# Two more K tiles turned by DMA, another set turned by VectorE, and side work and weight loads moved: one attention kernel on one Trainium2 core

## The chip, the cores and the metric

The kernel runs on one core of one Trainium2 chip. The time is device microseconds from the start to the end of the program. Eleven runs of the kernel before had a median of 185.6 us (184.96 to 186.39). One further execution was recorded by the hardware profiler; it took 186.5 us, of which 183.6 us lie between its first and its last instruction (its span). All times of the trace count from the start of that span.

In what follows "turn" means transposing a K tile. TensorE (PE in the profile) multiplies matrices, ScalarE (ACT) computes the exponentials, VectorE (DVE) and GpSimd (POOL) copy and move, SyncE (SP) issues nearly all DMAs.

## What is computed

Attention over a window of a K/V cache, with a projection in front (`wq`) and one behind (`wo`). All data is bfloat16.

```python
B, Sq, D = 8, 32, 1024
Hq, Hkv, Sk, Dh = 32, 4, 8192, 128
W = min(4096, max(256, Sk // 4))              # 2048
rep = Hq // Hkv                               # 8 query heads share one K/V head
q = (x @ wq).reshape(B, Sq, Hq, Dh).transpose(0, 2, 1, 3)
k = jnp.repeat(k_cache[:, :, Sk - W:, :], rep, axis=1)
v = jnp.repeat(v_cache[:, :, Sk - W:, :], rep, axis=1)
p = softmax(einsum("bhqd,bhkd->bhqk", q, k) * Dh ** -0.5)
o = einsum("bhqk,bhkd->bhqd", p, v)
out = o.transpose(0, 2, 1, 3).reshape(B, Sq, Hq * Dh) @ wo
```

The kernel reads 16.8 MB of K, 16.8 MB of V, 8.4 MB of `wq` and 8.4 MB of `wo`.

## The kernel before

**Units, chunks, slots.** A unit is one pair of batch and K/V head: 32 units, numbered 0 to 31, all eight batches of head 0 first. A unit has 256 queries (8 heads by 32 positions) and 2048 keys. Its keys are taken in four chunks of four key tiles (128 keys each), so the main loop (`run`, L445) has 128 chunks. Their number is also called the slot: chunk `c` of unit `u` is slot `4u + c`.

**One slot on TensorE.** Four score matmuls (`s_ps`, L467: 128 keys by 256 queries each); then the eight matmuls of probabilities by V (`o_ps`, L478) of the chunk two slots earlier; then the side work that a plan puts into this slot. ScalarE turns each chunk's scores into `pT` with one exponential of 128 by 1024 (L469). There are two score buffers and two output accumulators, so TensorE can run at most two chunks ahead of ScalarE. V is copied by VectorE into a wider tile `va` with a column of ones (`va_copy`, L409), so that the sum of the softmax comes out of the same matmul. When a unit is done, `finish_unit` (L411) takes the reciprocal, scales (two instructions, L420) and transposes (L422) into `OT`, all on VectorE.

**Four ways to turn K.** The score matmul needs K with the head dimension on the partitions. `load_k` (L178) and the plan choose per unit:

- units 0 to 4 (`PE_T`, L24): a plain load of 512 KB, then 16 transposes on TensorE (`k_pieces`, L224; L236) and two VectorE copies out of PSUM (L238); unit 0 is turned in `start`;
- units 5, 8, 11, ... 29 (`V_T`, L26): a plain load, four block transposes on VectorE (L251), then 16 moves of 32 by 512 (`kv_pieces`, L241). The last number of an entry of `V_T` says how many of the 16 moves are GpSimd's (L261): 12 for unit 5, 16 for the others; VectorE makes the rest (L259). The first number says behind which unit's loads the plain load is issued, the middle ones in which slots the block transposes and the moves stand;
- the other 18 units: two transposing DMAs of 256 KB each (L196), the first eight key tiles and the last eight, one before V's load and one behind it.

**Loads.** All these DMAs go through SyncE's one queue in the order in which `load_unit` (L207) issues them: K, V, K's second half, then the plain K loads that `V_T` ties to this unit, then the weight pieces that `W_AT` (L28) ties to it. `load_unit` stands in the program five units ahead of use, but SyncE does not follow the slots: it goes on as fast as its waits on buffers and on the queue let it. V has 6 buffers, turned K of the transposing DMA 5, weight tiles 6.

**Weights and projections.** A weight piece is 512 KB, half of a tile; there are 28 behind the start (12 of `wq`, 16 of `wo`), listed in the order of use (L332 to L338). A tile of `wq` holds four of the eight row groups `c` of all eight heads of one K/V head, so that each contiguous run in memory is 1024 elements, 2 KB. The projection of the next head group's queries is side work: 16 pieces of four matmuls (`q_pieces`, L267), a VectorE copy after every second one (L278); `Q_SLOTS` (L30) says over which slots they are spread evenly. The output projection of a finished head group is 16 pieces of two matmuls (`o_pieces`, L282), spread by `O_SLOTS` (L31); pieces planned for slots from 128 on run after the loop.

**The start.** `start` (L312) loads x and the eight row groups of `wq` of head group 0, and multiplies each with all eight heads when it has landed (L375). For row groups 0 to 5 all 256 queries are done at once; for 6 and 7 (`Q_CUT`, L19) only the first 128, and the other half follows in slots 0 and 1 of the loop (`q_rest`, L401).

What moves and what stays can be read in these lines of the plan:

```python
for ui, (_, s0, s1, s2, _) in V_T.items():
    blocks, moves = self.kv_pieces(ui)
    for k, p in enumerate(blocks):
        plan[s0[k]].append(p)
    spread(moves, s1, s2)
```

Of the kernel before, what the change touches and what calls it, by code (L numbers as in the profile page):

```python
# [9 lines left out]
ALU = mybir.AluOpType  # L10
# [5 lines left out]

RL_LIMIT = 1.0e22
RL_MIN = 1.0e-10
Q_CUT = 6  # L19
N_WARM = (8, 0, 0)  # L20
VA_ROW = 160
V_HALVES = 30

PE_T = (0, 1, 2, 3, 4)  # L24

V_T = {5: (2, (5, 6, 8, 10), 10, 17, 12),  # L26
       **{u: (u - 4, range(4 * u - 16, 4 * u - 12), 4 * u - 13, 4 * u - 4, 16) for u in (8, 11, 14, 17, 20, 23, 26, 29)}}
W_AT = (3, 3, 4, 4, 8, 8, 9, 9, 11, 12, 13, 13, 14, 15, 16, 16, 18, 19, 19, 20, 22, 22, 23, 24, 25, 26, 28, 28)  # L28

Q_SLOTS = {1: (17, 31), 2: (38, 54), 3: (69, 83)}  # L30
O_SLOTS = {0: (54, 71), 1: (84, 101), 2: (99, 123), 3: (124, 143)}  # L31


@with_exitstack
# [70 lines left out]
class Fast:  # L105
# [50 lines left out]
    def load_wq(self, g, half, cuts=(2, 2)):  # L156
# [8 lines left out]
                                   in_=self.wq[:, g * GW:(g + 1) * GW].rearrange("(p c) n -> p c n", p=P)[:, c0:c0 + n, :])  # L165
        return [lambda i=sum(cuts[:k]), n=n: piece(i, n) for k, n in enumerate(cuts)]

    def load_wo(self, gq):

        def piece(i):  # L170
            if i == 0:
                self.wo_t[gq] = self.wp.tile([self.P, 4, self.D], BF16, name="wo_sb", tag="w")
            r0 = gq * 4 * self.Dh
            self.nc.sync.dma_start(out=self.wo_t[gq][:, 2 * i:2 * i + 2, :],
                                   in_=self.wo[r0:r0 + 4 * self.Dh, :].rearrange("(p c) n -> p c n", c=4)[:, 2 * i:2 * i + 2, :])
        return [lambda i=i: piece(i) for i in range(2)]
# [30 lines left out]
    def load_unit(self, ui):  # L207

        if ui < len(self.units):
            if ui not in V_T:  # L210
                self.load_k(ui, None if ui in PE_T else 0)
            self.load_v(ui, self.nc.sync)
            if ui not in V_T and ui not in PE_T:
                self.load_k(ui, 1)
        for u, at in V_T.items():
            if at[0] == ui:
                self.load_k(u)
        for p, at in zip(self.weights, W_AT):
            if at == ui:
                p()  # L220

# [17 lines left out]
    def kv_pieces(self, ui):  # L241


        nc, P, KT = self.nc, self.P, self.KT
        st = {}

        def blocks(i):
            if i == 0:
                st["kb"] = self.kbp.tile([P, KT, P], BF16, name="kb")
            sl = slice(i * KT // 4, (i + 1) * KT // 4)  # L250
            nc.vector.transpose(out=st["kb"][:, sl, :], in_=self.k_raw[ui][:, sl, :])  # L251

        def move(k, d):
            if k == d == 0:
                self.kT[ui] = self.kvt.tile([P, KT, P], BF16, name="kTv", tag="kv")
            out = self.kT[ui][d * 32:(d + 1) * 32, :, k * 32:(k + 1) * 32]
            in_ = st["kb"][k * 32:(k + 1) * 32, :, d * 32:(d + 1) * 32]
            if d >= V_T[ui][4] // 4:
                nc.vector.tensor_copy(out=out, in_=in_)  # L259
            else:  # L260
                nc.gpsimd.tensor_scalar(out=out, in0=in_, scalar1=1.0, scalar2=1.0, op0=ALU.mult, op1=ALU.mult)  # L261
        return [lambda i=i: blocks(i) for i in range(4)], [lambda k=k, d=d: move(k, d) for k in range(4) for d in range(4)]
# [4 lines left out]
    def q_pieces(self, g):  # L267
        nc, P, DC = self.nc, self.P, self.DC
        st = {}

        def piece(hl, i):
            if i == 0:
                st["ps"] = self.ps_m.tile([P, 512], FP32, name="q_ps", tag="m")
            for c in range(i * DC // 2, (i + 1) * DC // 2):
                nc.tensor.matmul(st["ps"][:, 0:self.NQ], lhsT=self.wq_t[g, i][:, c % (DC // 2), hl * P:(hl + 1) * P],  # L275
                                 rhs=self.xT[:, c, :], start=(c == 0), stop=(c == DC - 1))
            if i == 1:
                nc.vector.tensor_copy(out=self.q_view(g)[:, :, hl, :],  # L278
                                      in_=st["ps"][:, 0:self.NQ].rearrange("p (b s) -> p b s", b=self.B))
        return [lambda h=h, i=i: piece(h, i) for h in range(self.rep) for i in range(2)]  # L280

    def o_pieces(self, g, t, cuts=(512, 512), st=None):  # L282

# [28 lines left out]
    def start(self):  # L312
# [15 lines left out]
        self.load_k(0, 1)  # L328
        self.load_v(0, nc.sync)
        self.load_k(1)  # L330
        self.load_v(1, nc.sync)
        self.weights = []  # L332
        for g in range(self.Hkv):
            if g + 1 < self.Hkv:
                self.weights += self.load_wq(g + 1, 0) + self.load_wq(g + 1, 1)
            if g:
                self.weights += self.load_wo(2 * g - 2) + self.load_wo(2 * g - 1)
        self.weights += self.load_wo(2 * self.Hkv - 2) + self.load_wo(2 * self.Hkv - 1)  # L338
        for ui in range(2, 4):
            self.load_unit(ui)  # L340
        for v in self.va:
            nc.gpsimd.memset(v[:, :, self.Dh:self.VW], 1.0)
        nc.gpsimd.memset(self.ones_c[:, :], 1.0)
        def warm_up(n):
            for i in range(n):
                nc.tensor.matmul(warm[:, :], lhsT=one(1.0, [P, P], BF16), rhs=one(1.0, [P, 512], BF16), start=True, stop=True)
        warm_up(N_WARM[0])


        def x_turn(half, pl, tag):  # L350
# [4 lines left out]
            for i, copy in ((0, nc.vector.tensor_copy), (1, nc.scalar.copy)):  # L355
# [2 lines left out]

        x_turn(0, self.ps_m, "m")
        x_turn(1, self.ps_s, "s_ps")  # L360
        qs = [pl.tile([P, 2, self.NQ], FP32, name="q0_ps", tag=tag)
              for pl, tag in ((self.ps_o, "o_ps"), (self.ps_o, "o_ps"), (self.ps_m, "m"), (self.ps_m, "m"))]
        KT = self.KT
        tp = None

# [4 lines left out]
        def k_copy(half):  # L370
            sl = slice(half * KT // 2, (half + 1) * KT // 2)
            nc.vector.tensor_copy(out=self.kT[0][:, sl, :], in_=tp[:, sl, :])

        def q_mm(c, h, n0, n1):
            nc.tensor.matmul(qs[h // 2][:, h % 2, n0:n1], lhsT=self.wq_t[0, c // H][:, c % H, h * P:(h + 1) * P],  # L375
                             rhs=self.xT[:, c, n0:n1], start=(c == 0 and h % 2 == 0), stop=(c == self.DC - 1),
                             skip_group_check=True)

        for c in range(self.DC):
            for h in range(self.rep):  # L380
                q_mm(c, h, 0, P if c >= Q_CUT else self.NQ)
            if c == 0:
                warm_up(N_WARM[2])
                warm_sb = self.c1.tile([P, 8], BF16, name="warm_sb")
                nc.vector.tensor_copy(out=warm_sb[:, :], in_=warm[:, 0:8])
            if c == self.DC - 3:
                tp = self.ps_s.tile([P, KT, P], BF16, name="kf_ps", tag="s_ps")
                k_turn(0)
                k_copy(0)
        k_turn(1)  # L390

        def q_copy(eng, k, b0, b1):
            src = qs[k][:, :, :].rearrange("p h (b s) -> p b h s", b=self.B)[:, b0:b1, :, :]
            dst = self.q_view(0)[:, b0:b1, k * 2:(k + 1) * 2, :]
            (nc.vector.tensor_copy if eng == "v" else nc.scalar.copy)(out=dst, in_=src)
        for k, eng in ((0, "a"), (1, "v"), (2, "a"), (3, "v")):
            q_copy(eng, k, 0, 1)
        k_copy(1)
        self.va_copy(0)

        def q_rest(k):  # L401
            for h in (2 * k, 2 * k + 1):
                for c in range(Q_CUT, self.DC):
                    q_mm(c, h, P, self.NQ)
            q_copy("v", k, 1, self.B)
        self.q_rest = [lambda k=k: q_rest(k) for k in (0, 2, 3, 1)]

    def va_copy(self, ui):
        self.nc.vector.tensor_copy(out=self.va[ui % 3][:, :, 0:self.Dh], in_=self.v_sb[ui][:, :, :])  # L409
# [1 line left out]
    def finish_unit(self, ui, o_ps):  # L411
# [4 lines left out]
        if ui == len(self.units) - 1:  # L416
            self.check_units(ui, ui + 1)
        o_sb = self.ob.tile([P, QT_N, 4, 32], BF16, name="o_sb")
        for qt in range(QT_N):
            nc.vector.tensor_scalar(out=o_sb[:, qt, :, :], in0=o_ps[:, qt, 0:Dh].rearrange("p (i c) -> p c i", c=4),  # L420
                                    scalar1=rl[:, ui * QT_N + qt:ui * QT_N + qt + 1], scalar2=None, op0=ALU.mult)
        nc.vector.transpose(out=self.OT[:, g * QT_N:(g + 1) * QT_N, :, b * self.Sq:(b + 1) * self.Sq], in_=o_sb[:, :, :, :])  # L422
        if ui == len(self.units) - 2:
            self.check_units(0, ui + 1)
# [1 line left out]
    def side_plan(self):  # L426
# [4 lines left out]
        def spread(pieces, s0, s1):  # L431
            for k, p in enumerate(pieces):
                plan[s0 + (s1 - s0) * k // len(pieces)].append(p)
        for g, w in Q_SLOTS.items():
            spread(self.q_pieces(g), *w)
        for g, w in O_SLOTS.items():
# [8 lines left out]
    def run(self):  # L445
        nc, P, NCH, CJ, UQ, QT_N, KT = self.nc, self.P, self.NCH, self.CJ, self.UQ, self.QT_N, self.KT
        self.start()
        plan = self.side_plan()
        for i, p in enumerate(self.q_rest):
            plan[i // 2].append(p)  # L450
        pv_queue = []

        loads = {8: [4, 5, 6, 7], **{4 * (u - 5): [u] for u in range(8, len(self.units))}}
# [1 line left out]
        for ui, (b, g) in enumerate(self.units):  # L455
            nxt = self.k_pieces(ui + 1)
            va = self.va[ui % 3]
            if ui:
                self.va_copy(ui)
            q_u = self.QT[g][:, b * UQ:(b + 1) * UQ]  # L460
            acc = {}
            for c in range(NCH):
                for u in loads.get(ui * NCH + c, []):
                    self.load_unit(u)
                s_ps = self.ps_s.tile([P, CJ, UQ], FP32, name="s_ps")
                for jj in range(CJ):
                    nc.tensor.matmul(s_ps[:, jj, :], lhsT=self.kT[ui][:, c * CJ + jj, :], rhs=q_u, start=True, stop=True)  # L467
# [188 lines left out]
```

## Time and profile before

| what | value |
|---|---|
| median of 11 runs | 185.6 us (184.96 to 186.39) |
| the profiled execution | 186.5 us, span 183.6 us |
| granted TensorE clock | 1.00 throughout |
| TensorE busy | 178.6 us of the span, 97% |
| exponentials on ScalarE (L469) | 128 of 1025 ns; ScalarE busy 72% |
| VectorE, GpSimd busy | 114.8 us (63%), 94.7 us (52%) |
| moves on GpSimd (L261) | 140 of 670 ns |
| all DMA traffic | 51.72 MB, mean 282 GB/s |
| first score matmul | at 13.28 us |

The busy times come from the page's first part, the clock from the list of cores, the first score matmul from the timeline. A share of busy time is a mean over the whole span; the page's second part cuts the span into 40 slices of 4.59 us and gives a busy digit for each, where 9 means 90% or more. The DMA rows there are means over the core's 16 DMA engines. "To landing" is the time from the issue of a DMA to the moment its data is reported complete. Matmuls overlap each other in the pipeline, so the mean duration of one (220 ns for L478) is more than the distance from one to the next; that distance is read from the timeline, where eight matmuls of L478 move the next group on by 0.45 us.

### The profile page before, as it was taken

What the parts mean: (1) busy time and instruction counts of PE and PEld (TensorE: products, weight loads), DVE (VectorE), ACT (ScalarE), POOL (GpSimd) and SP (SyncE); (2) the same over time, 40 slices, a digit from 0 to 9 for tenths busy, and PEclk for the clock granted to TensorE, in tenths of its full rate; (3) what the DMA queues carried; (4) which work ended last, traced back from release to release, by engine and by line L of the source; (5) the groups of instructions that cost most, each with busy time, mean ns of one, the idle gap of its engine ahead of it and who ended that gap; (6) DMA issues with size and microseconds to landing.
All of it is one profiled execution on the core that took longest, in us unless ns stands there. A gap on an engine that the chain in (4) does not pass through costs nothing.

```text
span 183.6 us, 5041 instructions
## 1 busy us (share of the span) xinstructions
PE 178.6 (97%) x2041; PEld 153.6 (84%) x2057; DVE 114.8 (63%) x266; ACT 131.5 (72%) x133; POOL 94.7 (52%) x150
## 2 busy tenths in 40 slices
PE   8989999999999999999999999999999999999994
PEld 3889999999999999987878999988787888888843
DVE  0238899985585784685567558647755865365363
ACT  2208899777889777878787677787877888888800
POOL 2000009859939959929944980796299279600000
PEclk9999999999999999999999999999999999999999
DMA  5999999999998999999999999989999999990003
GB/s 189 336 411 406 399 401 377 147 271 385 263 341 264 338 294 321 402 255 246 373 384 234 377 390 232 249 318 383 250 370 342 219 279 264 223 213 0 0 31 91
DMA packets 52953, 51.72 MB, mean 282 GB/s; under 512 B 39744, under 2 KB 40256, under 8 KB 52928
## 3 DMA queue, kind: packets, MB, share of 16 engines
q1 hardware_dynamic: 52352, 50.90, 98.4%
q10 hardware_dynamic: 576, 0.49, 0.8%
q8 instruction: 15, 0.25, 0.5%
q14 instruction: 10, 0.08, 0.1%
HBM read 41.42 MB, written 0.52 MB: 228 GB/s over the span
## 4 chain that ended last, share of the span: by engine, by line
PE 93%; DMA 4%; SPq 1%; issue 1%; DVE 0%
PE o_ps L478 32%; PE s_ps L467 31%; PE op_ps L295 14%; PE q_ps L275 11%; DMA wq_sb<-in_wq_dram 4%; PE q_ps L375 2%; PE tp L236 2%; SPq L164 1%; PE kf_ps L368 1%; SPq L320 0%; DVE o_t L305 0%; PE cnt_ps L532 0%
## 5 line engine op out<-in xcount | busy, mean ns | idle before, releaser
L469 ACT ACTIVATE pT<-s_ps 128x1024 bf16<-128x1024 f32 x128 | 128.7, 1025 | 32.5 <-PE s_ps L467 31.5
L261 POOL TENSOR_SCALAR kTv<-kb 32x512 bf16<-32x512 bf16 x140 | 93.8, 670 | 64.2 <-PE s_ps L467 37.7
L478 PE MATMUL o_ps<-va,pT 128*128 128x129 bf16 x1024 | 78.8, 220 | 0.1
L478 PEld LDWEIGHTS <-pT 128*128 128x128 bf16 x1024 | 68.5, 98 | 3.1
L467 PE MATMUL s_ps<-QT,kT 128*128 128x256 bf16 x368 | 55.2, 272 | 0.2
L467 PEld LDWEIGHTS <-kT 128*128 128x128 bf16 x368 | 34.8, 98 | 10.3
L295 PE MATMUL op_ps<-wo_sb,OT 128*128 128x512 bf16 (+2 forms) x128 | 32.7, 352 | 0.6
L275 PE MATMUL q_ps<-xT,wq_sb 128*128 128x256 bf16 x192 | 28.2, 273 | 0.0
L409 DVE COPY va<-v_sb 128x2048 bf16<-128x2048 bf16 x32 | 25.3, 789 | 0.1
L251 DVE STREAM_TRANSPOSE kb<-k_raw 128x512 bf16<-128x512 bf16 x36 | 23.8, 684 | 0.0
L415 DVE RECIPROCAL RL_all<-o_ps 128x2 f32<-128x2 f32 x32 | 5.2, 164 | 27.5 <-PE o_ps L478 27.5
L467 PE MATMUL s_ps<-QT,kTv 128*128 128x256 bf16 x144 | 21.6, 272 | 0.0
L420 DVE TENSOR_SCALAR o_sb<-o_ps,RL_all 128x128 bf16<-128x128 f32 x64 | 19.5, 346 | 1.1
L467 PEld LDWEIGHTS <-kTv 128*128 128x128 bf16 x144 | 13.9, 98 | 5.1
L278 DVE CAST QT<-q_ps 128x256 bf16<-128x256 f32 x24 | 9.7, 406 | 13.4 <-PE q_ps L275 13.4
L275 PEld LDWEIGHTS <-wq_sb 128*128 128x128 bf16 x192 | 17.0, 98 | 1.2
L422 DVE STREAM_TRANSPOSE OT<-o_sb 128x256 bf16<-128x256 bf16 x32 | 14.3, 446 | 1.1
L295 PEld LDWEIGHTS <-OT 128*128 128x128 bf16 x144 | 11.4, 98 | 2.3 <-DVE OT L422 0.2
L302 DVE TENSOR_TENSOR oacc<-op_ps,oacc 128x512 f32<-128x512 f32 x8 | 5.5, 682 | 7.4 <-PE op_ps L295 7.4
L375 PE MATMUL q_ps<-xT,wq_sb 128*128 128x256 bf16 (+1 forms) x80 | 7.8, 251 | 0.6 <-DMA wq_sb<-in_wq_dram 0.6
L375 PEld LDWEIGHTS <-wq_sb 128*128 128x128 bf16 x80 | 6.6, 98 | 1.6 <-DMA wq_sb<-in_wq_dram 0.9
L236 PE MATMUL tp<-ident,k_raw 128*128 128x128 bf16 x64 | 5.9, 219 | 0.0
(30 smaller groups left out, 36.5 us busy)
## 6 DMA issues: line engine op xcount, KB each, us to landing
v_sb<-in_v_cache_dram SPq DMA_DIRECT2D x30, 512.0 KB, 7.3
wo_sb<-in_wo_dram SPq DMA_DIRECT2D x16, 512.0 KB, 6.4
wq_sb<-in_wq_dram SPq DMA_DIRECT2D x13, 512.0 KB, 7.3
k_raw<-in_k_cache_dram SPq DMA_DIRECT2D x13, 512.0 KB, 5.9
wq_sb<-in_wq_dram SPq DMA_DIRECT2D x6, 256.0 KB, 4.8
v_sb<-in_v_cache_dram SPq DMA_DIRECT2D x4, 256.0 KB, 5.3
kT<-in_k_cache_dram SPq DMA_TRANSPOSE x36, 6.9
k_raw<-in_k_cache_dram SPq DMA_DIRECT2D x2, 256.0 KB, 6.9
```

Of the source, the lines that this page charges most:

```text
L251: nc.vector.transpose(out=st["kb"][:, sl, :], in_=self.k_raw[ui][:, sl, :])
L261: nc.gpsimd.tensor_scalar(out=out, in0=in_, scalar1=1.0, scalar2=1.0, op0=ALU.mult, op1=ALU.mult)
L275: nc.tensor.matmul(st["ps"][:, 0:self.NQ], lhsT=self.wq_t[g, i][:, c % (DC // 2), hl * P:(hl + 1) * P], rhs=self.xT[:, c, :], start=(c == ...
L278: nc.vector.tensor_copy(out=self.q_view(g)[:, :, hl, :], in_=st["ps"][:, 0:self.NQ].rearrange("p (b s) -> p b s", b=self.B))
L295: nc.tensor.matmul(ps[:, 0:w], lhsT=self.OT[:, gq, c, t * P:(t + 1) * P], rhs=self.wo_t[gq][:, c, n0:n0 + w], start=(k == 0), stop=(k == 7))
L375: nc.tensor.matmul(qs[h // 2][:, h % 2, n0:n1], lhsT=self.wq_t[0, c // H][:, c % H, h * P:(h + 1) * P], rhs=self.xT[:, c, n0:n1], start=(c ...
L409: self.nc.vector.tensor_copy(out=self.va[ui % 3][:, :, 0:self.Dh], in_=self.v_sb[ui][:, :, :])
L420: nc.vector.tensor_scalar(out=o_sb[:, qt, :, :], in0=o_ps[:, qt, 0:Dh].rearrange("p (i c) -> p c i", c=4), scalar1=rl[:, ui * QT_N + qt:ui ...
L422: nc.vector.transpose(out=self.OT[:, g * QT_N:(g + 1) * QT_N, :, b * self.Sq:(b + 1) * self.Sq], in_=o_sb[:, :, :, :])
L467: nc.tensor.matmul(s_ps[:, jj, :], lhsT=self.kT[ui][:, c * CJ + jj, :], rhs=q_u, start=True, stop=True)
L469: nc.scalar.activation(out=pT[:, :, :], in_=s_ps[:, :, :], func=ACT.Exp, bias=0.0, scale=self.scale)
L478: nc.tensor.matmul(o_ps[:, qt, 0:self.VW], lhsT=pT[:, jj, qt * P:(qt + 1) * P], rhs=va[:, j, 0:self.VW], start=(j == 0 and qt == 0), stop= ...
```

## The change

- Units 3 and 4 leave `PE_T` and are loaded by transposing DMA. The set that VectorE turns is now 5, 9, 12, 15, ... 30 (nine units, as before), so 8, 11, 14, ... 29 become units of the transposing DMA. That kind has 20 units instead of 18.
- Every entry of `V_T` now has 12 moves on GpSimd and 4 on VectorE, in every fourth place of the 16. The slots of the moves and block transposes are new.
- `wq` of head groups 1 to 3 is loaded by heads: a tile holds all eight row groups of four heads. The contiguous run in memory is 512 elements, 1 KB. `W_AT` is new, and in `load_unit` the weight pieces go ahead of the plain K loads instead of behind them.
- In the start V1 is loaded behind K2, and K2, V2, K5 are named one by one. Row groups 0 to 7 are multiplied with all 256 queries for heads 0 to 3 and with the first 128 for heads 4 to 7; the other half of heads 4 to 7 is side work in slots 0 to 2 and 8 to 12 (`q_late`). The queries of heads 4 to 7 need one PSUM bank instead of two.
- `Q_SLOTS` and `O_SLOTS` are new. The last of the 16 pieces of `O_SLOTS[2]` falls on slot 128 and two others on slots 126 and 127; before, all 16 ended by slot 121.
- The query copies of head groups 1 to 3 move from VectorE (24 of 128 by 256) to ScalarE (12 of 128 by 512). The two scaling instructions of `finish_unit` become one. From unit 12 on `va_copy` stands in the last slot of the unit before.

```diff
-PE_T = (0, 1, 2, 3, 4)
-V_T = {5: (2, (5, 6, 8, 10), 10, 17, 12),
-       **{u: (u - 4, range(4 * u - 16, 4 * u - 12), 4 * u - 13, 4 * u - 4, 16) for u in (8, 11, 14, 17, 20, 23, 26, 29)}}
-W_AT = (3, 3, 4, 4, 8, 8, 9, 9, 11, 12, 13, 13, 14, 15, 16, 16, 18, 19, 19, 20, 22, 22, 23, 24, 25, 26, 28, 28)
-Q_SLOTS = {1: (17, 31), 2: (38, 54), 3: (69, 83)}
-O_SLOTS = {0: (54, 71), 1: (84, 101), 2: (99, 123), 3: (124, 143)}
+PE_T = (0, 1, 2)
+V_T = {5: (2, (6, 7, 8, 9), 10, 17, 12),
+       9: (5, range(22, 26), 25, 34, 12),
+       **{u: (u - 4, range(4 * u - 15, 4 * u - 11), 4 * u - 12, 4 * u - 3, 12) for u in range(12, 32, 3)}}
+W_AT = (3, 3, 5, 5, 8, 8, 10, 11, 12, 12, 13, 13, 17, 17, 19, 20, 21, 21, 22, 22, 25, 25, 26, 26, 28, 28, 29, 29)
+Q_LATE = {0: (0, 2), 1: (8, 12)}
+V_EARLY = 12
+Q_SLOTS = {1: (14, 31), 2: (36, 56), 3: (75, 93)}
+O_SLOTS = {0: (56, 75), 1: (93, 112), 2: (112, 130), 3: (124, 143)}
...
+    def load_wq_heads(self, g, half):
+        P, DC, GW = self.P, self.DC, self.rep * self.Dh
+        n0 = g * GW + half * GW // 2
+        def piece(i):
+            if i == 0:
+                self.wq_t[g, half] = self.wp.tile([P, DC, GW // 2], BF16, name="wq_sb", tag="w")
+            cs = slice(i * DC // 2, (i + 1) * DC // 2)
+            self.nc.sync.dma_start(out=self.wq_t[g, half][:, cs, :],
+                                   in_=self.wq[:, n0:n0 + GW // 2].rearrange("(p c) n -> p c n", p=P)[:, cs, :])
...
+        for p, at in zip(self.weights, W_AT):
+            if at == ui:
+                p()
         for u, at in V_T.items():
             if at[0] == ui:
                 self.load_k(u)
-        for p, at in zip(self.weights, W_AT):
-            if at == ui:
-                p()
...
-            if d >= V_T[ui][4] // 4:
+            i, n = 4 * k + d, 16 - V_T[ui][4]
+            if i * n // 16 != (i + 1) * n // 16:
                 nc.vector.tensor_copy(out=out, in_=in_)
...
+            for c in range(i * DC // 2, (i + 1) * DC // 2):
+                nc.tensor.matmul(st["ps"][:, hl % 2, :], lhsT=self.wq_t[g, hl // R][:, c, (hl % R) * P:(hl % R + 1) * P],
+                                 rhs=self.xT[:, c, :], start=(c == 0 and hl % 2 == 0), stop=(c == DC - 1), skip_group_check=True)
+            if i == 1 and hl % 2 == 1:
+                nc.scalar.copy(out=self.q_view(g)[:, :, 2 * k:2 * k + 2, :].rearrange("p b h s -> p h b s"),
+                               in_=st["ps"][:, :, :].rearrange("p h (b s) -> p h b s", b=self.B))
...
+    def q_late(self, h0):
...
+            for c in range(DC):
+                nc.tensor.matmul(st["ps"][:, i, :], lhsT=self.wq_t[0, c // (DC // 2)][:, c % (DC // 2), (h0 + i) * P:(h0 + i + 1) * P],
+                                 rhs=self.xT[:, c, P:self.NQ], start=(c == 0 and i == 0), stop=(c == DC - 1), skip_group_check=True)
             if i == 1:
-                nc.vector.tensor_copy(out=self.q_view(g)[:, :, hl, :],
-                                      in_=st["ps"][:, 0:self.NQ].rearrange("p (b s) -> p b s", b=self.B))
+                nc.vector.tensor_copy(out=self.q_view(0)[:, B // 2:, h0:h0 + 2, :].rearrange("p b h s -> p h b s"),
+                                      in_=st["ps"][:, :, :].rearrange("p h (b s) -> p h b s", b=B // 2))
...
-        self.load_v(1, nc.sync)
...
-        for ui in range(2, 4):
-            self.load_unit(ui)
+        self.load_k(2)
+        self.load_v(1, nc.sync)
+        self.load_v(2, nc.sync)
+        self.load_k(5)
+        self.load_unit(3)
...
-        for qt in range(QT_N):
-            nc.vector.tensor_scalar(out=o_sb[:, qt, :, :], in0=o_ps[:, qt, 0:Dh].rearrange("p (i c) -> p c i", c=4),
-                                    scalar1=rl[:, ui * QT_N + qt:ui * QT_N + qt + 1], scalar2=None, op0=ALU.mult)
+        nc.vector.tensor_tensor(out=o_sb[:, :, :, :], in0=o_ps[:, :, 0:Dh].rearrange("p q (i c) -> p q c i", c=4),
+                                in1=rl[:, ui * QT_N:(ui + 1) * QT_N].unsqueeze(2).unsqueeze(3).to_broadcast([P, QT_N, 4, 32]), op=ALU.mult)
...
-            if ui:
+            if 0 < ui < V_EARLY:
                 self.va_copy(ui)
...
+                if c == NCH - 1 and V_EARLY <= ui + 1 < len(self.units):
+                    self.va_copy(ui + 1)
```

## The prediction, made before the change was run

> **What bounds the kernel.** I read the sliced span first, then the chain that ended last, then windows by stage, then SyncE's timeline against TensorE's.
>
> ```profile
> PE   8989999999999999999999999999999999999994
> DMA  5999999999998999999999999989999999990003
> GB/s 189 336 411 406 399 401 377 147 271 385 263 341 264 338 294 321 402 255 246 373 384 234 377 390 232 249 318 383 250 370 342 219 279 264 223 213 0 0 31 91
> ```
> ```profile
> PE 93%; DMA 4%; SPq 1%; issue 1%; DVE 0%
> ```
>
> Two rows are full, not one. TensorE is at 9 from the fifth slice to the end, and the chain runs along it for 93%. But the DMA row is full too, until about 165 us, while its rate falls from 400 GB/s to between 147 and 402 once the transposing DMAs begin (31 us). So the DMA engines are busy with something other than bytes.
>
> ```profile
> core 0: us, PE busy (x) PEld busy (x) DVE busy (x) ACT busy (x) POOL busy (x), PEclk, DMA share, GB/s
> 17.50:22.50 5.00, 5.00 (x75) 4.79 (x73) 3.74 (x9) 4.36 (x5) 0.00 (x0) 1.00 1.03 405
> 94.00:110.00 16.00, 15.89 (x183) 13.95 (x184) 10.02 (x24) 11.52 (x12) 10.50 (x17) 1.00 1.10 341
> 142.00:165.00 23.00, 22.74 (x258) 19.04 (x261) 14.04 (x33) 19.27 (x20) 12.31 (x18) 1.00 1.10 244
> 9.00:165.00 156.00, 154.66 (x1827) 136.60 (x1841) 105.52 (x238) 120.93 (x122) 93.75 (x140) 1.00 1.12 313
> ```
>
> The first row has plain loads only: 405 GB/s. The last has everything: 156 us at 313 GB/s are 48.8 MB. The 36 transposed halves (262 KB each) are 9.4 of these; the other 39.4 MB at 405 GB/s take 97.3 us. The rest, 58.7 us, went to the 36 halves: **1.63 us each**, where 262 KB loaded plainly take 0.65. The same sum gives 1.28 in the 94 to 110 window (4 halves) and 1.95 in the 142 to 165 window (7 halves).
>
> How close the loads are to their use shows at the end:
>
> ```profile
> 152.44 1.00 SPq L204 DMA_DIRECT2D v_sb<-in_v_cache_dram  x2
> 153.50 6.36 SPq L196 DMA_TRANSPOSE kT<-in_k_cache_dram  x2
> 159.95 1.00 SPq L204 DMA_DIRECT2D v_sb<-in_v_cache_dram  x2
> 161.01 1.23 SPq L196 DMA_TRANSPOSE kT<-in_k_cache_dram  x1
> ```
> ```profile
> L196 SPq DMA_TRANSPOSE kT<-in_k_cache_dram x1: 1231/1231/1231, 161.0 to 161.0; - x1
> ...
> DMA to landing us min/median/max: 5.8/5.8/5.8
> ```
> ```profile
> 171.27 0.60 PE L467 MATMUL s_ps<-QT,kT 128*128 128x256 bf16 x4
> ```
>
> SyncE issues back to back, without a gap. The last half (K of unit 31) is issued at 161.0, lands at 166.8, and TensorE first needs it at 171.27: **4.5 us of slack** at the end of a queue that has been full for 160 us. Since DMA time added anywhere ahead of it moves this landing, this is the view that decides. The buffers (6 of V, 5 of K) would let SyncE run further ahead; it doesn't, so I read its pace as the queue's.
>
> **TensorE's sum.** Distances from the chain of waits:
>
> ```profile
> 13.88 0.45 PE q_ps L375 x8
> 16.16 0.45 PE tp L236 x8
> 34.85 0.44 PE q_ps L275 x4
> ```
>
> K3 and K4 leave: 32 transposes at 0.056 = -1.79 us. The start: 48 matmuls of 256 columns (0.109 each), 16 of 128 and 16 more in the loop become 32 of 256, 32 of 128 and 32 more in `q_late`. Ahead of the last `wq` piece TensorE waits for DMA anyway, so what it saves there is worth nothing; from row group 4 on the old order has 16x0.109 + 16x0.056 = 2.64 us, the new 16x0.109 + 16x0.056, the same, so the first score matmul stays at 13.28. In the loop 32 narrow ones stand where 16 stood: +0.90. Net **-0.9 us**. Three pieces of the output projection (0.44 each) move behind the last K's first use: TensorE then wants that half at 171.27 - 0.9 - 1.3 = 169.1, and has 12.3 + 1.3 = 13.6 us to do behind it.
>
> **The loads' sum.** Units with transposed K rise from 18 to 20, plain ones fall by two: 4 x (1.63 - 0.65) = **+3.9 us**. Ends: 4 x 0.63 = 2.5 and 4 x 1.30 = 5.2, by the two windows. The 12 `wq` pieces go from runs of 2 KB to 1 KB. The trace's load packets took a median 84 ns for 2 KB and 162 for 4 KB, a line that gives 45 for 1 KB; two of them are 7% over one of 2 KB. A 512 KB piece takes 524/405 = 1.29 us, so 12 x 0.09 = **+1.1 us**. Low end 0; high end 2.2, by the 1 KB packets that are in the trace (48 ns, but those are output stores). Together +5.0. The last half lands at 171.8 instead of 169.1: 2.7 us late, less the 0.9 gained: **+1.8 us**. Check: 171.8 + 13.6 = 185.4 of span against 183.6. Outside the span lie 2.9 us, so the profiled execution would be 188.3; the median is 0.9 under the profiled one, hence **187.4**.
>
> The loss would come sooner than unit 31. Unit 13's first half had 6.0 us of slack (landed 70.4, used 76.4). By unit 14 the new order has nine transposed units against six: 6 x 0.98 = 5.9 us, plus 0.7 for eight `wq` pieces, less TensorE's 0.9 earlier. So the first wait of TensorE on a K half should be near unit 13 or 14; the waits are not added up, the latest decides.
>
> At such a wait everything behind the score matmul on TensorE's queue stands: the V matmuls, side work, and with them ScalarE and `finish_unit`.
>
> The skill speaks for the change here: "Advanced Engine Details and Errata", section "X-Bar Transpose (TRN2)", says transposing DMAs are as fast as ordinary ones. The rows above say 1.63 against 0.65 us. By the page the four halves would cost nothing and the time would be an estimated 184.7; by the row it is 187.4. "DMA: Bandwidth & Descriptors", section "Latency and other measured facts", gives 261 GB/s for a non-contiguous transposing DMA, an estimated 1.0 us a half, between the two.
>
> **What costs nothing, and what covers it.**
>
> ```profile
> L278 DVE CAST QT<-q_ps 128x256 bf16<-128x256 f32 x24 | 9.7, 406 | 13.4 <-PE q_ps L275 13.4
> L420 DVE TENSOR_SCALAR o_sb<-o_ps,RL_all 128x128 bf16<-128x128 f32 x64 | 19.5, 346 | 1.1
> L259 DVE COPY kTv<-kb 32x512 bf16<-32x512 bf16 x4 | 1.8, 450 | 0.1
> L469 ACT ACTIVATE pT<-s_ps 128x1024 bf16<-128x1024 f32 x128 | 128.7, 1025 | 32.5 <-PE s_ps L467 31.5
> ```
>
> ScalarE takes 12 query copies; its nearest rows are 588 ns (128x512, bf16) and 212 (128x64 from PSUM), so 0.2 to 0.9 each, I take 0.6: 7 us inside its 32.5 us of idle time. With side work a slot takes TensorE 1.33 us, ScalarE 1.03; one copy delays an exponential by about 0.3 and two score buffers hold that. Without cover it would be 7 us. VectorE loses 24 x 0.41, four K copies (2.7) and one of two scalings per unit (0.27 x 32, against the 425 ns of a 128x256 sum from PSUM), and gains 32 moves x 0.45 = 14.4: about 6.5 us less of 114.8. GpSimd loses 32 x 0.67. Neither was at its limit. Slots 32 to 35 without side work take 0.89 on TensorE against ScalarE's 1.03; the old kernel had seven such slots in a row with TensorE still full.
>
> **Rivals.**
>
> *The loads keep up* (the other side). If a half costs 1.28 us or less, as it did from 94 to 110, and 1 KB runs cost nothing, the additions are 2.5 us, the last half lands at 169.3, and the TensorE sum stands: 185.6 - 0.9 = **184.7**. It decides below 2.3 us of added DMA time. For it: the rate differs by window, and part of the 1.63 may be stalls that another order avoids; more weight pieces now stand between transposed pairs late in the run. Against it: the pattern half, V, half is unchanged.
>
> *VectorE is held at its own queue's head.* K12 is now issued behind unit 8's halves and two weight pieces, three loads or 3.9 us after a half that unit 8 itself needs in slot 34, while its first block transpose stands in slot 33. VectorE would stand up to 4.8 us, then do four blocks (2.7), and only then `va_copy` of unit 9 (0.79): 2.5 us too late for slot 38. Its later kin are covered by `va_copy`'s earlier place, at 0 to 0.5 each for six units. Price 2.5 + 1.5 over the gain: **188.5** (187.2 without the later ones). For it: the load stands close; against: VectorE has idle time in slots 34 to 36. It decides when K12 lands over 2.3 us after slot 33.
>
> *Loads late by just the gain*: 0.9 us, **185.6**. Also the outcome if the evened side work does nothing and the K halves are covered.
>
> **How the numbers follow.** Loads late 0.51 (own range 186.0 to 189.8; 5.2 + 2.2 = 7.4 us of additions give 189.8); loads keep up 0.29; VectorE held 0.10; near balance 0.10. Under 0.2% (0.37 us) no difference can be told in this kernel. Slower 0.61, same 0.10, faster 0.29. The range runs from the TensorE sum with 0.3 to spare, 184.4, to 189.8.
>
> **What would show it.** Right: TensorE waits for `kT` from the transposing DMA, first near unit 13, some 2 to 4 us in all; last transposed half landing near 172; a half at 1.5 us or more by the same sum of windows; no wait for ScalarE. Wrong: TensorE full and the last landing before 169, or waits put down to `va` or `wq`.

## The result and the profile after

The changed kernel takes 188.4 us (median of 13 runs, 187.0 to 191.5) against 185.7 for the kernel before, run beside it: a ratio of 1.0121, 95% interval 1.0099 to 1.0143. It is slower, by 2.2 us by that ratio and by 2.7 by the medians. (Ratios leave out disturbed runs, so here and below they can lie under the quotient of two medians.) Its profiled execution took 189.35 us, with a span of 187.6 (183.6 before).

The sliced span of the changed kernel, in slices of 4.69 us:

```profile
PE   8899999999995999999999999999999999999993
PEclk9999999999999699999999999999999999999999
DMA  5999999998999999999999999999999999992012
GB/s 193 347 411 393 216 264 349 321 268 168 248 356 251 343 357 271 351 263 336 224 295 312 274 311 382 281 259 318 256 374 300 390 263 216 373 324 50 0 47 76
```

The DMA row is full as before, from the second slice to about 168 us; the rate now falls from 400 GB/s in the fifth slice (K3 and K4); before, it fell in the eighth. New are a 5 in TensorE's row, at 56 to 61 us, and a 6 in the row of its granted clock right behind it. These two digits are most of what this execution lost. The chain that ended last now runs along DMAs for 12%, where it was 4%:

```profile
PE 81%; DMA 12%; SPq 3%; DVE 1%; issue 1%; DVEq 0%
```

The waits of the changed kernel (total us, how often, longest) say where:

```profile
DVE va L440 <- DMA v_sb<-in_v_cache_dram: 13.6, 9, 2.6
...
DVE kb L266 <- DMA k_raw<-in_k_cache_dram: 5.5, 3, 2.9
...
PE o_ps L510 <- DVE va L440: 2.2, 2, 2.0
...
PEld L499 <- DMA kT<-in_k_cache_dram: 0.7, 1, 0.7
```

TensorE waits for VectorE's copy of V, and VectorE waits for plain loads. VectorE's timeline (start, length, line, work, idle time before it in brackets), then TensorE's:

```profile
54.40 0.54 DVE L275 COPY kTv<-kb 32x512 bf16<-32x512 bf16 x1
57.81 1.90 DVE L266 STREAM_TRANSPOSE kb<-k_raw 128x512 bf16<-128x512 bf16 x3 [2.87 <-DMA k_raw<-in_k_cache_dram]
59.63 0.65 DVE L440 COPY va<-v_sb 128x2048 bf16<-128x2048 bf16 x1
```
```profile
57.73 0.60 PE L499 MATMUL s_ps<-QT,kTv 128*128 128x256 bf16 x4
60.34 0.67 PE L510 MATMUL o_ps<-va,pT 128*128 128x129 bf16 x8 [2.00 <-DVE va L440]
60.80 1.06 PE L292 MATMUL q_ps<-xT,wq_sb 128*128 128x256 bf16 x4
61.65 1.06 PE L499 MATMUL s_ps<-QT,kTv 128*128 128x256 bf16 x4
...
64.20 0.60 PE L499 MATMUL s_ps<-QT,kT 128*128 128x256 bf16 x4
```

K12's plain load landed at 57.72. VectorE had stood at K12's first block transpose since 54.94; behind that, in its queue, stood the V copy of unit 9, which TensorE wanted in slot 38. TensorE lost 2.00 us. But V9 itself landed only at 58.98 (51.56 before): without K12 ahead of it the copy would have started 0.65 us earlier, no more. A third of the wait is VectorE's order, two thirds are the late load. Then its matmuls ran at half pace until 64.2: a group of four took 1.06 us instead of 0.60, and the next group began 0.85 us behind it instead of 0.43. The windows of the changed kernel show the clock:

```profile
core 0: us, PE busy (x) PEld busy (x) DVE busy (x) ACT busy (x) POOL busy (x), PEclk, DMA share, GB/s
48.00:58.00 10.00, 9.99 (x126) 9.23 (x124) 4.08 (x10) 9.70 (x11) 6.22 (x10) 1.00 1.21 298
58.00:60.30 2.30, 0.33 (x4) 0.15 (x2) 2.30 (x5) 1.15 (x2) 0.00 (x0) 1.00 0.74 233
60.30:64.20 3.90, 3.86 (x28) 3.15 (x28) 3.77 (x7) 1.02 (x1) 2.87 (x5) 0.56 1.18 336
...
31.00:170.00 139.00, 135.89 (x1551) 118.36 (x1562) 92.52 (x184) 112.73 (x121) 68.24 (x102) 0.99 1.13 300
```

At a clock of 0.56 those 3.9 us do the work of 2.2: another 1.7 us. TensorE looks busy there (3.86 of 3.90), so the busy row alone hides this loss. The last row is most of the stretch with transposing DMAs: full at 300 GB/s.

The fall of the clock belongs to this execution, not to the kernel's usual time. Over the whole span the granted clock was 0.990 here and 0.993 in one other (191.5 us) of the 15 executions whose clock is on record; in the other 13 it was 0.998 or more, and the execution with the median time of 188.4 us, with a span of 186.6, had 1.00.

**Where this execution's 4.0 us of span come from.** I summed the distances between successive matmuls behind the first score matmul, less what their columns take at full pace. This excess grew by 4.66 us: 2.0 and 1.7 at 58 to 64 us, 0.4 in a wait for `va` at 152.4, 0.3 in one for `kT` at 159.8, and 0.3 in smaller pieces. TensorE's own work fell by 0.86, the first score matmul came 0.22 earlier (13.06), and what follows the last matmul took 0.37 longer: 4.66 - 0.86 - 0.22 + 0.37 = 3.95.

The end, which the prediction had made decisive, is no longer it. SyncE's queue, then TensorE:

```profile
162.83 1.02 SPq L219 DMA_DIRECT2D v_sb<-in_v_cache_dram  x2
163.91 3.10 SPq L211 DMA_TRANSPOSE kT<-in_k_cache_dram  x1
```
```profile
173.57 0.60 PE L499 MATMUL s_ps<-QT,kT 128*128 128x256 bf16 x4
```

The last half landed at 171.60 and was used at 173.57: the time already lost at 58 to 64 us covers it.

The rows that the prediction had costed, in the profile after (busy time, mean ns; idle before):

```profile
L440 DVE COPY va<-v_sb 128x2048 bf16<-128x2048 bf16 x32 | 26.7, 835 | 14.2 <-DMA v_sb<-in_v_cache_dram 13.6
...
L275 DVE COPY kTv<-kb 32x512 bf16<-32x512 bf16 x36 | 18.0, 499 | 0.8
...
L450 DVE TENSOR_TENSOR o_sb<-o_ps,RL_all 128x256 bf16<-128x256 f32 x32 | 13.6, 424 | 1.1
...
L295 ACT CAST QT<-q_ps 128x512 bf16<-128x512 f32 x12 | 7.0, 580 | 0.6 <-PE q_ps L292 0.6
```

None of these is where the time went, except that `va` waits for loads 13.6 us in all; TensorE in turn waited 2.2 us for `va` (the row of `o_ps` in the waits above).

### The profile page after: what moved, and what is told of

It is laid out like the page before. It is cut to its first block, busy times and chain, and to the rows that moved or that the text cites. A ratio compares the mean times of both kernels' runs of the same rounds, so it can differ in the third digit from the quotient of the medians.

```text
span 187.6 us, 4971 instructions
## 1 busy us (share of the span) xinstructions
PE 179.8 (96%) x2026; PEld 153.8 (82%) x2041; DVE 117.2 (62%) x238; ACT 136.2 (73%) x145; POOL 73.4 (39%) x118
## 4 chain that ended last, share of the span: by engine, by line
PE 81%; DMA 12%; SPq 3%; DVE 1%; issue 1%; DVEq 0%
PE o_ps L510 27%; PE s_ps L499 27%; PE op_ps L327 13%; PE q_ps L292 10%; DMA k_raw<-in_k_cache_dram 4%; DMA kT<-in_k_cache_dram 4%; DMA wq_sb<-in_wq_dram 3%; PE q_ps L410 2%; DVE kb L266 1%; PE ql_ps L307 1%; PE tp L251 1%; SPq L166 1%; SPq L211 1%; SPq L179 1%; PE kf_ps L402 0%
## 5 line engine op out<-in xcount | busy, mean ns | idle before, releaser
L277 POOL TENSOR_SCALAR kTv<-kb 32x512 bf16<-32x512 bf16 x108 | 72.5, 671 | 89.0 <-DVE kb L266 43.4
L440 DVE COPY va<-v_sb 128x2048 bf16<-128x2048 bf16 x32 | 26.7, 835 | 14.2 <-DMA v_sb<-in_v_cache_dram 13.6
L292 PE MATMUL q_ps<-xT,wq_sb 128*128 128x256 bf16 x192 | 29.7, 278 | 0.0
L275 DVE COPY kTv<-kb 32x512 bf16<-32x512 bf16 x36 | 18.0, 499 | 0.8
L292 PEld LDWEIGHTS <-wq_sb 128*128 128x128 bf16 x192 | 17.2, 100 | 1.3
L450 DVE TENSOR_TENSOR o_sb<-o_ps,RL_all 128x256 bf16<-128x256 f32 x32 | 13.6, 424 | 1.1
L295 ACT CAST QT<-q_ps 128x512 bf16<-128x512 f32 x12 | 7.0, 580 | 0.6 <-PE q_ps L292 0.6
L410 PE MATMUL q_ps<-xT,wq_sb 128*128 128x256 bf16 (+1 forms) x64 | 5.9, 249 | 0.6 <-DMA wq_sb<-in_wq_dram 0.6
L410 PEld LDWEIGHTS <-wq_sb 128*128 128x128 bf16 x64 | 5.1, 100 | 1.2 <-DMA wq_sb<-in_wq_dram 0.8
```

The costliest lines, as they stand in the source:

```text
L292: nc.tensor.matmul(st["ps"][:, hl % 2, :], lhsT=self.wq_t[g, hl // R][:, c, (hl % R) * P:(hl % R + 1) * P], rhs=self.xT[:, c, :], start=(c ...
L410: nc.tensor.matmul(ps, lhsT=self.wq_t[0, c // H][:, c % H, h * P:(h + 1) * P], rhs=self.xT[:, c, 0:n], start=(c == 0 and h in (0, 2, 4)), ...
L450: nc.vector.tensor_tensor(out=o_sb[:, :, :, :], in0=o_ps[:, :, 0:Dh].rearrange("p q (i c) -> p q c i", c=4), in1=rl[:, ui * QT_N:(ui + 1) ...
```

## The experiments

Theory: the loads are late; what waits first is secondary. Rival: only the one hold of VectorE at K12 costs time, and the loads would do.

**The price of a transposed half, by itself.** A kernel that only issues loads (a "half" is one transposing DMA of 256 KB, half of a unit's K): six plain ones; four units of half, V, half; three of half, V, half and two plain; six halves in a row; eight weight pieces in 2 KB and 1 KB runs. Nothing is computed, the output is zeros.

```diff
+        for u in range(4):
+            h = turned(u)
+            h(0)
+            plain(6 + u, "v_a")
+            h(1)
```

> Loads alone, nothing computed (the output is zeros): 6 plain loads of V; four units as half, V, half; three units as half, V, half and two plain loads; three units as half, half; four weight pieces in runs of 2 KB, four in runs of 1 KB; one plain load. If the price of a transposed half belongs to the queue itself: a unit (half, V, half) takes 1.3 + 2 x 1.6 = 4.5 us from landing to landing, against 1.3 for a plain 512 KB load, and the stalls are there with all engines idle. If it comes from the engines that work beside it: a half takes 0.9 or less, a unit 3.0 us. 1 KB runs: 1.5 us a piece against 1.3 (7 to 14% more); no difference if the run length does not matter.

Its windows: the four units, then those with plain loads between them, then the six halves:

```profile
core 0: us, DVE busy (x) POOL busy (x), PEclk, DMA share, GB/s
11.00:28.00 17.00, 0.00 (x0) 0.00 (x0) 1.00 1.13 255
28.00:46.00 18.00, 0.00 (x0) 0.00 (x0) 1.00 1.11 299
46.00:58.00 12.00, 0.00 (x0) 0.00 (x0) 1.00 1.06 254
```

The last halves of the four units landed 4.20 us apart on average (from 10.72, the landing of the load before them, to 27.52 in four steps); a plain 512 KB took 1.28, so a half took 1.46. In the second group it was 1.50 on average, though two of the three units took only 5.7 us (0.95 a half). Six in a row took 1.25 each. No engine computes here, so most of the price of 1.63 us belongs to the loads themselves, not to the engines' work beside them. 1 KB pieces took 1.50 each; 2 KB pieces 1.4 to 2.25, too uneven for a price.

**K12 later** (the block transposes of unit 12 four slots later, its moves four to two slots later):

```diff
-       **{u: (u - 4, range(4 * u - 15, 4 * u - 11), 4 * u - 12, 4 * u - 3, 12) for u in range(12, 32, 3)}}
+       **{u: (u - 4, range(4 * u - 15, 4 * u - 11), 4 * u - 12, 4 * u - 3, 12) for u in range(12, 32, 3)},
+       12: (8, range(37, 41), 40, 47, 12)}
```

> The changed kernel, with unit 12's block transposes in slots 37 to 40 instead of 33 to 36 and its moves in 40 to 47: the loads are untouched, and VectorE copies V of unit 9 before it waits for K12. If the held VectorE is the loss: the 2.0 us wait at 58 us and the slow clock behind it go, and the time falls by 3 to 4 us to 184.5 to 185.5. If the loads as a whole are too late: TensorE reaches unit 13 and 14 some 4 us earlier, whose halves had 1.7 and 0.3 us of slack, and waits there for kT from the transposing DMA; the time stays at 187 to 188.5.

Measured 188.9 us (186.6 to 190.8), ratio 1.0108 [1.0073, 1.0143]: no gain that can be told over the changed kernel (1.0121). The waits of its trace, an execution of 189.75 us:

```profile
PE s_ps L500 <- DMA kT<-in_k_cache_dram: 2.2, 1, 2.2
...
PE o_ps L511 <- DVE va L441: 1.2, 1, 1.2
PE s_ps L500 <- DVE kTv L276: 1.1, 1, 1.1
```

K12 no longer stood ahead of V9's copy, but V9 landed at 58.68 and the copy began 0.02 us later; K12's moves were late in their turn, and at unit 14 TensorE waited 2.2 us for K itself (landed 84.75).

**K ahead of the weights** (the old order of these two in `load_unit`):

```diff
-        for p, at in zip(self.weights, W_AT):
-            if at == ui:
-                p()
         for u, at in V_T.items():
             if at[0] == ui:
                 self.load_k(u)
+        for p, at in zip(self.weights, W_AT):
+            if at == ui:
+                p()
```

> The changed kernel, with the plain K loads of VectorE's units ahead of the weight pieces again, as before the change. K12 is issued two weight pieces (3.1 us) earlier. If the held VectorE is the loss: as above, 184.5 to 185.5. If the loads as a whole are too late: the wait moves to kT of units 13, 14, 23 or 29, or to a weight tile, and the time is 187 to 188.5.

Measured 188.2 us (4 runs), ratio 1.0153 [1.009, 1.0216]; span of the profiled execution 185.8.

```profile
PE s_ps L499 <- DMA kT<-in_k_cache_dram: 1.8, 2, 1.7
...
PE o_ps L510 <- DVE va L440: 0.4, 1, 0.4
```

K12 now landed at 53.07 and the hold was gone, and the clock stayed at 1.0. What came instead is the wait that the prediction had named: on K13's second half (landed 0.05 us before its use) and on both halves of K14 (1.7 us for the first).

The rival falls here, by two kernels: without the hold the time is no better (four runs, 187.6 to 190.0, here; ten with K12 later), and the wait moves to where the loads are late.

**K3 and K4 on TensorE again, the rest of the change kept:**

```diff
-PE_T = (0, 1, 2)
+PE_T = (0, 1, 2, 3, 4)
```

> The changed kernel, with units 3 and 4 turned by TensorE again (plain loads). TensorE gets 1.8 us more work, the load queue 3 to 4 us less. If the loads are what costs: everything lands 3 to 4 us earlier, K12 and K14 too, no wait over 0.5 us is left, and TensorE's sum gives 185.7 - 0.9 + 1.8 = 186.6. If the loss lies in the new places of side work or in ScalarE's copies: the waits stay and the time is 189 to 190.

Measured 186.9 us (186.8 to 187.4), ratio 1.0065 [1.0044, 1.0086]. TensorE waits for no K or V load (K14's halves landed 0.94 and 1.16 us ahead), and the runs lie within 0.6 us of each other where the changed kernel's spread over 4.5. What is left over the kernel before is the work of `q_late` and two short waits for VectorE's copies of K out of PSUM, at 25 and 31 us:

```profile
PE tp L251 <- DVE kT L253: 0.7, 1, 0.7
...
PE q_ps L292 <- DVE kT L253: 0.4, 1, 0.4
```

**K3 and K4 loaded plainly, not turned at all** (their scores are then of other numbers; every instruction but the four loads is the changed kernel's):

```diff
+            if ui in (3, 4):
+                nc.sync.dma_start(out=self.kT[ui][:, part * H:(part + 1) * H, :],
+                                  in_=src.rearrange("(p j) d -> p j d", j=KT)[:, part * H:(part + 1) * H, :])
+                return
             nc.sync.dma_start_transpose(out=self.kT[ui][:, part * H:(part + 1) * H, :],
```

> The changed kernel, with the four halves of K3 and K4 loaded plainly into the same tiles (K of units 3 and 4 stays unturned, so their scores are those of another matrix). Bytes, places in the queue, and all work of the engines are as in the change; only the kind of these four DMAs differs. If the price of the four transposed halves is what costs: everything behind them lands 3 to 4 us earlier, VectorE is held at K12 for less than 0.5 us, the waits near unit 14 shrink below 0.5 us, and TensorE's sum gives 184.8 to 185.6. If the runs of 1 KB, the order of the queue or the side work cost as much: 186.5 to 188.5.

Measured 186.2 us (184.5 to 189.1), ratio 1.0017 [0.9983, 1.005]. Span of the profiled execution 183.4, and the row of TensorE is full from the third slice on; VectorE waits for K12 no more:

```profile
PE   8899999999999999999999999999999999999993
```

So the four transposing DMAs alone make 2.2 of the 2.7 us by the medians, and 1.9 of the 2.2 us by the ratios. The rest of the change, with these four at the price of plain loads, makes no difference that can be told. It is no gain either: the median lies 0.6 us above the 184.8 to 185.6 that TensorE's sum gave. The loads have no slack left even so: K14's second half landed 0.05 us ahead of its use.

**The same edit on the kernel before:** K3 and K4 by DMA, and K4 alone.

```diff
-PE_T = (0, 1, 2, 3, 4)
+PE_T = (0, 1, 2)
```

> The kernel before, with units 3 and 4 loaded by transposing DMA and nothing else changed. TensorE loses 1.8 us of work, the loads gain 3 to 4 us. If the loads decide: their slack (3.0 us at unit 10, 4.5 at the end) is used up or just exceeded, TensorE waits 0 to 1.5 us for kT at unit 10 or in the last units, and slots 8 to 15 without side work leave it up to 0.6 us for ScalarE: 184.6 to 186.0. If transposing DMAs were as cheap as plain ones: 183.9 to 184.5.

> The kernel before, with unit 4 alone loaded by transposing DMA. TensorE loses 0.9 us, the loads gain 1.5 to 2 us, less than their slack by every row. Expected by all theories: 184.7 to 185.1, no wait of TensorE. If it is not faster, the slack of the loads is not what the landings say.

Both: 191.4 us (six runs, 186.9 to 193.2), ratio 1.0107 [1.0031, 1.0182]. K4 alone: 186.0, ratio 1.0013 [0.9991, 1.0036], no difference. Both expectations were missed: the slack read from the landings did not hold the added loads. The sliced span and the waits of the first, in an execution of 191.45 us, 4.6 more than the shortest of the six:

```profile
PE   8999997299999999999999999999999999999993
PEclk9999999659999999999999999999999999999999
```
```profile
PE q_ps L275 <- DMA wq_sb<-in_wq_dram: 4.7, 2, 2.4
```

Without the moved weights the delay of the loads meets `wq` of head group 1, at 31.6 and 34.3 us, and the clock falls behind it. With K4 alone TensorE waits 0.46 us for `wq` (at 33 us) and 0.37 us for `va` of unit 3 (28.7 us), which together (0.83) cancel the 0.9 us that it saves.

**Half, half, V instead of half, V, half**, since six halves in a row had been cheaper:

```diff
-            self.load_v(ui, self.nc.sync)
             if ui not in V_T and ui not in PE_T:
                 self.load_k(ui, 1)
+            self.load_v(ui, self.nc.sync)
```

> The changed kernel, with each transposed unit loaded as half, half, V instead of half, V, half; bytes, packets and everything else as in the change. Loads alone gave 1.25 us for a half that follows another half, 1.46 to 1.50 in the pattern half, V, half. If the price of the transposed halves is what makes the change slower: the 40 halves cost some 9 us less (40 x 0.23), the last half lands before 166 us, no wait of TensorE for a load over 0.5 us is left, and TensorE's sum stands: 184.5 to 185.2. If another cost decides (side work, ScalarE's copies, the later V): 187.5 to 189, whatever the landings do.

> The changed kernel with half, half, V and K2 by transposing DMA as well (the late queries of heads 6 and 7 then in slots 5 and 7). TensorE loses another 0.9 us. If the cheaper order leaves the loads slack: 183.7 to 184.4. If the loads decide again: a wait for kT by unit 13 or 14 and 185 or more.

The first took 197.4 us, ratio 1.0618 [1.0555, 1.068]; the second, with K2 by DMA as well, 196.4, ratio 1.0575 [1.0532, 1.0617]. The expectation failed by 12 us. From the waits of the first:

```profile
DVE va L440 <- DMA v_sb<-in_v_cache_dram: 40.5, 15, 5.0
...
PE s_ps L499 <- DMA kT<-in_k_cache_dram: 5.2, 4, 1.8
```

The halves did not get cheaper: by the sum of windows they cost 1.85 us each (34 to 168 us; 1.65 in the changed kernel). SyncE stood at the issue of a second half for as long as 7.5 and 5.2 us (13.4 to 20.8, 34.0 to 39.1), V landed 2 to 4 us later behind the pair, and the last half at 178.4. Why pairs are dearer here, when six in a row alone were cheaper, isn't shown.

**V from another engine's queue**, to see whether SyncE's issue or the transfer paces the halves: V of units 4 to 31 on GpSimd's, then on ScalarE's.

```diff
-            self.load_v(ui, self.nc.sync)
+            self.load_v(ui, self.nc.scalar if ui > 3 else self.nc.sync)
```

> The changed kernel, with V of units 4 to 31 issued by GpSimd on its own queue instead of SyncE's. If SyncE's issue of descriptors sets the pace of the transposed halves: V's bytes flow beside it, the last half lands before 166 us, and the time is 184.8 to 185.6. If the DMA engines themselves are the limit: the landings stay, 187.5 to 189. GpSimd is idle 60% of the time but issues behind its moves; if its own issue is late or slow, V is late and the time is over 190.

> The changed kernel, with V of units 4 to 31 issued by ScalarE on its queue. Same two cases for the landings: 184.8 to 185.6 if SyncE's issue sets the pace, 187.5 to 189 if the DMA engines do. An issue takes ScalarE 0.4 to 0.5 us, 28 of them 13 us of its 30 us idle; if it is held by a full queue, its exponentials wait and the time is over 190.

225.7 us (216.5 to 231.2) and 220.9 us (ratio 1.1857 [1.1788, 1.1926]). Both are inconclusive for their question: the engine that issues V is held by the waits of its issues. On ScalarE, which in the 11.8 us of the last row issued three loads of V and nothing else:

```profile
PE s_ps L499 <- ACT pT L501: 26.1, 6, 11.1
...
ACT pT L501 <- DMA kT<-in_k_cache_dram: 11.8, 1, 11.8
```

**What might keep the gain:** the kernel before with K4 by DMA, the weights of unit 4 ahead of K8's load, K8's turn two slots earlier, and the scaling in one instruction.

```diff
-PE_T = (0, 1, 2, 3, 4)
+PE_T = (0, 1, 2, 3)
...
-        **{u: (u - 4, range(4 * u - 16, 4 * u - 12), 4 * u - 13, 4 * u - 4, 16) for u in (8, 11, 14, 17, 20, 23, 26, 29)}}
+        **{u: (u - 4, range(4 * u - 16, 4 * u - 12), 4 * u - 13, 4 * u - 4, 16) for u in (11, 14, 17, 20, 23, 26, 29)},
+        8: (4, range(18, 22), 21, 30, 16)}
```

> The kernel before with K4 alone loaded by transposing DMA, the weight pieces of unit 4 put ahead of the K load at that unit, VectorE's turn of K8 two slots earlier, and the scaling of finish_unit in one instruction. Theory (the loads' slack decides): K4 by DMA takes 0.9 us from TensorE and 1 us of the loads' lead (two halves at 1.63 less two plain ones at 0.65 is 2.0 us, before the weight pieces move ahead). In b2_k4_dma this was cancelled by a wait of 0.46 us for a weight piece at 33 us and one of 0.37 us for va at 28.7 us. Here the piece is issued ahead of the two transposed halves of K8's load step and so lands over 1 us earlier, and VectorE saves some 0.27 us a unit: both waits go, 184.7 to 185.2. Rival (the lead is used up anyway): the wait only moves to the K and V of units 9 to 14, whose slack in b2_k4_dma was 0.26 to 1.03 us, and the time is 185.7 to 186.3.

Measured 185.6 us (12 runs) against 185.4, ratio 1.0018 [0.9987, 1.005]: no difference; neither expectation's account is right. The two waits for `wq` and `va` went as foreseen. Half of the 0.9 us came back as two short waits for GpSimd's moves of K5 (35.4 us) and K8 (51.6 us):

```profile
PEld L472 <- POOL kTv L267: 0.6, 2, 0.3
```

They take 0.23 and 0.28 us on TensorE. The last matmul ended 0.45 us earlier than before (180.44 against 180.89), the last store landed 0.46 us earlier, and the span was 183.6 all the same: what follows the last store took 1.3 us instead of 0.9.

## Why the prediction was right, and where it was not

The forecast, loads late, holds: 188.4 against 187.4, inside its own range. But its route differed. Of the signs that it had named, the last landing (171.6) and the price of a half came. The wait of 2 to 4 us for `kT` did not: in the changed kernel's trace TensorE waits 0.2 us for it, and the wait that came is put down to `va`, one of the signs for "wrong". With K ahead of the weights the wait for `kT` is there, at units 13 and 14.

- **TensorE's sum** (-0.9): -0.86 by its columns, and 0.22 for the first score matmul, which the prediction had left in place.
- **The halves' price** (+3.9): the cause is shown by the two kernels that differ in these loads alone. Loaded plainly, the last half lands at 166.9 instead of 171.6 (4.7 us); turned on TensorE, at 168.6 (3.0 us); both differences carry the scatter told in the next point. The same sum over the changed kernel (the row from 31 to 170 us, 36 halves) gives 1.65, against 1.63; alone it is 1.25 to 1.50.
- **The last landing** (171.8): 171.6, but this agreement is better than the method, and so partly luck. With the plain K loads ahead of the weights, the same bytes through the same queue, it was 168.4; with K12 later, 170.95; before, with K4 alone by DMA, 165.8, a microsecond earlier than without. From single executions the sum is good to some 2 or 3 us, not to 0.2. What makes the difference stays open.
- **The middle of the run:** loads 6.6 us later by unit 14, and the first wait on K at unit 13 or 14. K13's first half landed 5.7 us later and V14 5.5. In the changed kernel TensorE was late by then and K14 came 0.28 us ahead of its use; with K ahead of the weights the wait is exactly there.
- **"The waits are not added up, the latest decides", with 13.6 us behind the last half.** This step failed. The last half was no longer waited for (it landed 1.97 us ahead of its use), because TensorE had already lost 3.7 us at 58 to 64. They began in slot 38 with a wait of 2.0 us, the place of the rival "VectorE is held at its own queue's head" (2.5 us, chance 0.10). The rival's condition was met, too: K12 landed 5.5 us after slot 33 began (52.19), where it asked for 2.3. But only 0.65 of the wait is that hold; the rest is V9, a load that the prediction had not looked at. That the rival's 188.5 (its own terms add up to 188.7) lies nearest to the 188.4 is luck: without the hold the time stays. K12, V9, K13 and K14 all come late; the first one on TensorE's path takes the loss, and the time that it costs gives slack to those behind it.
- **The slow clock** (1.7 us) was not in the sum, and did not have to be: it is in the profiled execution, not in the median one. Without it and with the wait where it was expected, the span is 185.8 (K ahead of the weights), 185.4 in the prediction; but the median of 188.2 there is no better than the changed kernel's.
- **Span and rest.** The prediction's 187.4 is a span of 185.4 and 2.0 us outside it (2.9 less the 0.9 by which the median lies under the profiled execution). The median execution had a span of 186.6 and 1.8 outside. So the span came out 1.2 us longer than the sum; as that execution has no trace, where these 1.2 us lie isn't known.
- **What was costed at nothing** was: ScalarE's query copies 580 ns (0.6 taken) with no wait of TensorE for them, the scaling 424 ns (425), the moves on VectorE 499 ns (450). VectorE did not get lighter, though: 117.2 us busy instead of 114.8, where 6.5 less was forecast. The moves took 1.6 us more than their price, the V copies 1.4 (835 ns each, 789 before), and the two scalings had overlapped (0.61 us for both in the timeline before), so that one in their place saved 0.19 a unit and not 0.27: 2.7 us. Most of the other 3.2 us is overlap between instructions of different lines: it hid 7.1 us of VectorE's work before and 4.1 after (the sum of the lines' busy times less the engine's).
- **1 KB runs** (+1.1): with K3 and K4 back on TensorE the last half lands 1.8 us later than in the kernel before. The second piece of a `wq` pair landed 1.3 to 2.4 us behind the first (1.3 to 1.5 before); 1 KB packets took a median 48 ns, 2 KB ones 84, which is the upper of its two ends (2.2). The landings, good to 2 or 3 us, cannot tell it from the 1.1 taken.

## What to carry to other kernels

Where two resources are full, an edit that moves work from one to the other has to be priced in the receiver's row; TensorE's 1.8 us of transposes cost the loads 3 to 5 us here, by the last landings of single executions. A load that is issued later has to be followed into the queue of the engine that waits for it: what stands behind that wait is late too. And when loads are late throughout, taking away the wait that the profile shows only moves it to the next one, so test the cause (the loads) and not the wait. And a loss read from one trace has to be held against the other executions: here 1.7 of its 4.0 us, the slow clock, are not in the median execution.

## What the runs showed of the hardware

- **A wait of 2.0 us was followed by 3.9 us at a mean clock of 0.56.** With waits of 2.4 and 2.3 us close together (K3 and K4 by DMA in the kernel before) the clock fell as well; with one of 2.2 us (K12 later) it didn't. The Trainium skill, "TensorE: Matmul & The Clock Gate", section "Part 1: The HAM clock gate", puts the half rate behind at least one idle window of about 3.4 us; here 2.0 us were enough in one execution and 2.2 not in another.
- **In no group of loads measured here was a transposed half as cheap as a plain one,** not even with nothing else running: 1.25 to 1.50 us on average, 0.95 at the least, against 0.64 (half of 1.28). This differs from "Advanced Engine Details and Errata", section "X-Bar Transpose (TRN2)", which the prediction had set aside for the trace.
- **Part of the price comes in stretches.** In the changed kernel's trace there are 17 stretches of 0.5 to 2.3 us, 22.6 us in all, in which 256-byte packets took over 350 ns, each while SyncE was issuing a transposing DMA with another one not yet landed, which is so in 59% of the time from 17 to 168 us. The kernels with the order half, V, half and V on SyncE's queue have 16 to 20 of them, with 22 to 26 us. Of the 40 halves' extra (40 times 0.98, 39 us) they are more than half in length. But the kernel before, with 36 halves, has 19 of them and 24.1 us, so they do not grow with the number of halves. Why they arise isn't shown.
